# A planned linear-attention and Fourier-mixing kernel: new load lengths in its plan, and the stored order of work and choice of engines made anew

## The chip, the core and the metric

The kernel runs on one core of a Trainium2 chip. The metric is device time in microseconds (us) of one execution. The kernel before takes 182.72 us, the median of three runs (182.53 to 183.22). About 0.5% of that, 0.9 us, is what a measurement of this kernel can tell from no change.

## The reference

Two stages follow each other, on 4 batches of 768 positions and 8 heads of 48 columns (384 columns in all). The first is a linear attention with a decaying state, the second a Fourier mixing of the whole batch and a two-layer network.

```python
for t in range(S):                                   # S = 768
    cur = einsum('bhd,bhe->bhde', u[None] * kt, vt)
    y[:, :, t] = einsum('bhd,bhde->bhe', rt, state + cur)
    state = wt[:, :, :, None] * state + einsum('bhd,bhe->bhde', kt, vt)
x = y as (batch, position, 384)
mixed = real(fft(fft(x, axis=1), axis=2))
u = x + mixed
un = (u - mean(u)) / sqrt(var(u) + 1e-06)            # over the 384 columns
out = u + maximum(un @ w_ch1, 0.0) @ w_ch2           # 384 -> 1536 -> 384
```

Inputs and output are float32; the kernel multiplies in bfloat16.

## The kernel before

**Tiling.** A batch is cut into six chunks of 128 positions, so that a tile is 128 positions by 384 columns. Chunk c of batch b is written (b, c) here. For each chunk, SP loads four tiles: `w`, `k`, `r` and `v`, of 192 KB each (`load_one`, L606). Seven buffers of each kind are used in turn. That makes 96 loads. The bonus `u` is one small load, the two network weights come in three large transfers issued by POOL (`weights`, L742).

**Attention** (`attention(b, c)`, L757). ACT takes the logarithm of `w` (tile `lb`), PE sums it along the positions by two matmuls with triangular masks (L773, L777), ACT exponentiates both sums (L779, L792). DVE multiplies `r` by one (L811) and DVE or POOL multiply `k` by the other (`rkh`, recorded by the helper line L561). Both are transposed on PE (L827, L833) and copied out of the accumulators (`rkt`). In batch 3 a DMA transposes them. PE multiplies them (L843), DVE masks the product (`ah`, L848), PE multiplies it with `v` and adds the state's part (L896, L899). The diagonal term goes a side way: `rk` = r times k, times u, a row sum (`dc`, L800), times v (`vtd`). The result is a row block of `x`. PE, DVE and at times ACT move the state to the next chunk (L869, L877, tile `st`).

**Fold** (`fold`, L914). Sums and differences of `x` (tiles `sd`, `xf`), on DVE or POOL, put it into the even and odd parts that halve the transform.

**Mixing and network** (`mix(b)`, L944). PE multiplies the folded tiles with cosine and sine tables (L965 to L968), the results are copied (`hcs`) and mirrored (`hcr`), and multiplied with the second table (L992). DVE adds `x` and takes row sums (L997). ACT or DVE make the centred tile `un`, which is transposed (`unt`). Two halves of three row blocks then go through the network: 12 groups of three matmuls of 128x384 (L1056), each followed by the rectifier that writes `ht` either on ACT (L1064) or on DVE (L1062), and 12 matmuls for each row block (L1075), scaled and added by DVE (`osb`, L1081) and stored by SP (L1085).

**What sets the order.** The program is recorded as 1450 numbered steps. `ORDER` (L40) holds for each engine the numbers of its steps, in the order in which it runs them; the list in which a number stands is also the choice of engine, for steps that have a choice. Each engine runs its list strictly in order, and waits on semaphores where a step needs something from another engine. `schedule` (L205) walks through these lists with planned lengths of steps. It decides three things that reach the chip: which of the eight accumulator banks a tile gets, the waits which follow from a bank's reuse, and some waits of POOL on DVE. It does not change the lists. The planned length of a load is `xfer=960` ns (L611), and the same number marks the loads for the rule that no more than four are under way in the plan (L240 and L293).

```python
L240    if e == "sp" and o.sem is not None and len(lds) >= 4:
L241        s = max(s, lds[-4].end - 100)
L293    if o.xfer == 960:
L294        lds.append(o)
```

PE also runs 36 matmuls without use (`warm`, steps 1414 to 1449, L1130), placed by the list between useful ones. All stand ahead of the first network matmul. The kernel opens with 16 more on a memset tile (L1098).

**Overlap.** The lists weave the stages of neighbouring batches: while batch b is in attention, PE runs the mixing and network of batch b - 1 between its steps.

Of the kernel before, what the change touches and what calls it, by code (L numbers as in the profile page):

```python
# [66 lines left out]
    "act": (  # L67
# [14 lines left out]
    "dve": (  # L82
# [61 lines left out]
class _Prog:  # L144
# [60 lines left out]
    def schedule(self, order):  # L205
# [19 lines left out]
        for left in range(len(self.ops)):  # L225
            best = None
            for e in self.ENGS:
                if at[e] == len(self.order[e]):
                    continue
                o = self.order[e][at[e]]  # L230
# [9 lines left out]
                if e == "sp" and o.sem is not None and len(lds) >= 4:  # L240
                    s = max(s, lds[-4].end - 100)  # L241
# [48 lines left out]
            elif o.sem is not None:  # L290
                t = self._land(max(hw[-1][3] if hw else 0, s + o.set), o.xfer, sw)
                hw.append([s + o.set, o.xfer, o, t])
                if o.xfer == 960:  # L293
                    lds.append(o)  # L294
# [869 lines left out]
```

## Time and profile before

| | |
|---|---|
| median of three runs | 182.72 us (182.53 to 183.22) |
| profiled execution: own time | 184.21 us |
| its span, first to last instruction | 182.4 us |
| granted TensorE clock | 1.00 |
| bytes moved by DMA | 28.99 MB |

The profile comes from one execution. The span is what the profile's rows add up to; 1.8 us of that execution lie outside it. Times of rows count from the start of the span. A group of instructions stands in one row: source line, engine, operation, tiles and shapes, how often, then busy time and the mean duration of one instruction in ns, then the idle time of the engine ahead of them and what ended most of it. Instructions of DVE and ACT overlap a little at their ends, so that the mean duration is longer than the distance of two starts. "PE" rows show matmuls, whose ends are modelled. Where the trace shows a helper's line (L561 for a product or sum of two tensors, L575 for an activation, L586 and L587 for copies out of the accumulators), the tile's name tells which step it is.

### The profile page before, as it was taken

The numbers are of one execution on the slowest core, as the hardware profiler recorded it, in microseconds if no ns is written. First come the engines' busy times: TensorE is split into PE (matmuls) and PEld (weight loads), VectorE is DVE, ScalarE is ACT, GpSimd is POOL, SyncE is SP. The second block draws the span as 40 slices with busy tenths as digits, with TensorE's granted clock in tenths as the row PEclk, the third lists the DMA queues.
The fourth block names the chain that finished last, engine by engine and source line by source line (L and its number), as shares of the span: only waits on it lengthen the run. The fifth ranks groups of instructions, "written<-read, shape, count | busy, mean of one in ns | idle before, by whom it ended". The sixth has DMA issues, their size and how long they took to land.

```text
span 182.4 us, 4568 instructions
## 1 busy us (share of the span) xinstructions
PE 176.8 (97%) x1722; PEld 116.3 (64%) x1722; DVE 148.2 (81%) x341; ACT 130.2 (71%) x340; POOL 101.5 (56%) x120
## 2 busy tenths in 40 slices
PE   7999999999999999999999999999999999999994
PEld 3465676766566666776657666656666676666663
DVE  8779999899899999999888997899979927622343
ACT  2889859597898675799899978888882247478200
POOL 2448789767231498589998968769653440000000
DMA  4999998999999899999999999997550103331214
GB/s 97 203 216 196 208 191 172 185 202 208 152 196 190 162 210 230 226 204 182 202 222 218 219 177 207 220 212 179 103 114 0 47 2 65 73 125 43 86 71 145
DMA packets 116119, 28.99 MB, mean 159 GB/s; under 512 B 111361, under 2 KB 116098, under 8 KB 116098
## 3 DMA queue, kind: packets, MB, share of 16 engines
q1 hardware_dynamic: 114514, 26.36, 70.2%
q0 software_dynamic: 1584, 2.36, 8.0%
q8 instruction: 13, 0.21, 0.5%
q14 instruction: 8, 0.07, 0.1%
HBM read 23.59 MB, written 4.72 MB: 155 GB/s over the span
## 4 chain that ended last, share of the span: by engine, by line
PE 61%; DVE 17%; DMA 9%; SPq 4%; ACT 4%; issue 3%; DVEq 0%
PE bank L1075 18%; PE bank L1056 17%; DMA in_w<-in_w_dram 5%; DMA w<-in_moe_w_ch_dram 4%; DVE ah L848 4%; SPq L609 4%; PE bank L992 3%; PE bank L1130 3%; PE bank L1098 3%; PE bank L968 3%; DVE osb L1081 2%; PE bank L843 2%; DVE rkh L561 2%; PE bank L889 2%; PE bank L899 2%
## 5 line engine op out<-in xcount | busy, mean ns | idle before, releaser
L1075 PE MATMUL bank<-w,ht 128*128 128x384 bf16 (+2 forms) x300 | 53.7, 320 | 0.0
L1056 PE MATMUL bank<-unt,w 128*128 128x384 bf16 x288 | 51.9, 326 | 0.6 <-DMA w<-in_moe_w_ch_dram 0.6
L1064 ACT ACTIVATE ht<-bank 128x384 bf16<-128x384 f32 x72 | 32.6, 496 | 9.3 <-PE bank L1056 8.9
L1056 PEld LDWEIGHTS bank<-unt,w 128*128 128x128 bf16 x288 | 26.9, 98 | 17.5 <-DVE ht L1062 0.8
L1075 PEld LDWEIGHTS bank<-w,ht 128*128 128x128 bf16 x300 | 27.5, 98 | 15.2
L848 DVE TENSOR_TENSOR ah<-bank,msk 128x512 bf16<-128x512 f32 x48 | 31.2, 682 | 2.1 <-PE bank L843 2.0
L561 POOL TENSOR_TENSOR rk<-rk,ub 128x384 f32<-128x384 f32 x21 | 21.6, 1034 | 8.6 <-DVE rk L561 7.0
L561 POOL TENSOR_TENSOR vtd<-in_v,dc 128x384 f32<-128x384 f32 x20 | 16.7, 837 | 11.2 <-DVE dc L800 8.1
L1081 DVE SCALAR_TENSOR_TENSOR osb<-bank,rstd,uf 128x384 f32<-128x384 f32 (+2 forms) x25 | 14.8, 596 | 9.5 <-PE bank L1075 5.9
L1062 DVE TENSOR_SCALAR ht<-bank 128x384 bf16<-128x384 f32 x24 | 13.0, 549 | 6.9 <-PE bank L1056 6.8
L561 POOL TENSOR_TENSOR rk<-in_r,in_k 128x384 f32<-128x384 f32 x17 | 16.9, 999 | 2.9 <-DMA in_r<-in_r_dram 1.4
L997 DVE SCALAR_TENSOR_TENSOR uf<-bank,x 128x384 f32<-128x384 f32 x24 | 12.5, 553 | 4.7 <-PE bank L992 4.6
L561 POOL TENSOR_TENSOR rkh<-in_k,e 128x384 bf16<-128x384 f32 x14 | 14.1, 1009 | 3.6 <-ACT e L792 2.0
L779 ACT ACTIVATE bank<-bank 128x384 f32<-128x384 f32 x24 | 11.5, 484 | 5.8 <-PE bank L773 5.8
L811 DVE TENSOR_TENSOR rkh<-bank,in_r 128x384 bf16<-128x384 f32 x24 | 13.1, 549 | 2.1 <-ACT bank L779 2.0
L575 ACT ACTIVATE xf<-uf,agg 128x384 bf16<-128x384 f32 x24 | 14.7, 614 | 0.0
L561 POOL TENSOR_TENSOR xf<-sd 128x382 bf16<-128x382 f32 (+1 forms) x10 | 10.6, 1062 | 6.5 <-DVE sd L561 3.0
L575 ACT ACTIVATE lb<-in_w 128x384 bf16<-128x384 f32 x24 | 12.4, 519 | 2.1 <-DMA in_w<-in_w_dram 1.8
L575 ACT ACTIVATE un<-uf,agg 128x384 bf16<-128x384 f32 x18 | 10.6, 611 | 4.1 <-DVE uf L997 4.1
L586 ACT ACTIVATE rkt<-bank 128x256 f32<-128x256 f32 x29 | 10.8, 389 | 3.6 <-PE bank L833 2.4
L561 POOL TENSOR_TENSOR sd<-x 128x385 f32<-128x385 f32 x10 | 10.0, 1015 | 5.9 <-DVE x L908 5.4
L792 ACT ACTIVATE e<-bank 128x392 f32<-128x392 f32 (+1 forms) x24 | 11.7, 497 | 2.3 <-DVE bank L877 1.0
(138 smaller groups left out, 358.7 us busy)
## 6 DMA issues: line engine op xcount, KB each, us to landing
in_w<-in_w_dram SPq DMA_DIRECT2D x24, 192.0 KB, 3.8
in_k<-in_k_dram SPq DMA_DIRECT2D x24, 192.0 KB, 3.8
in_r<-in_r_dram SPq DMA_DIRECT2D x24, 192.0 KB, 4.1
in_v<-in_v_dram SPq DMA_DIRECT2D x24, 192.0 KB, 4.0
out_dram<-osb SPq DMA_DIRECT2D x23, 192.0 KB, 2.8
w<-in_moe_w_ch_dram POOLq DMA_DIRECT2D x2, 576.0 KB, 8.1
w<-in_moe_w_ch_dram POOLq DMA_DIRECT2D x1, 1152.0 KB, 10.7
out_dram<-osb SPq DMA_DIRECT2D x1, 128.0 KB, 1.7
```

The lines of the kernel that those rows point to most:

```text
L561: return lambda e: e.tensor_tensor(out=o, in0=a, in1=b, op=f)
L575: return lambda e: e.activation(o, a, f, **kw)
L779: op("act", a_ps(DM) + 20, lambda e: e.activation(ps(tce)[:, 0:DM], ps(tce)[:, 0:DM], ACTF.Exp), w=[tce])
L792: op("act", a_ps(ne), lambda e: e.activation(E2[i2][:, 0:ne], ps(tci)[:, 0:ne], ACTF.Exp), r=[tci], w=[("E2", i2)])
L811: op("dve", v_1(DM), lambda e: e.tensor_tensor(out=rh[:, :, 0:D], in0=ps(tce)[:, 0:DM].rearrange("t (h d) -> t h d", d=D), in1=rt[:, :, :] ...
L848: masked[n] = op("dve", v_1(512), lambda e, x=x: e.tensor_tensor(out=ah[:, x:H:2, :], in0=ps(ta[x])[:, :].rearrange("p (h t) -> p h t", t= ...
L997: op("dve", v_1(DM) + 60, lambda e, kb=kb, t=t: e.scalar_tensor_tensor(out=uf[:, kb, :], in0=ps(t)[:, 0:DM], scalar=1.0, in1=xb[:, kb, 0:D ...
L1056: ins = e.matmul(ps(t)[:, 0:384], W1[:, m, 256 * (j // 2) + j % 2:256 * (j // 2) + 256:2], unt[:, :, m, :], start=(m == 0), stop=(m == NM ...
L1062: {"dve": lambda e, j=j, t=t, ht=ht: e.tensor_scalar(out=ht[:, j, :], in0=ps(t)[:, 0:384], scalar1=su, scalar2=0.0, op0=ALU.mult, op1=ALU. ...
L1064: "act": lambda e, j=j, t=t, ht=ht: e.activation(ht[:, j, :], ps(t)[:, 0:384], ACTF.Relu, scale=su)},
L1075: ins = e.matmul(ps(t)[:, 0:hi - lo], ht[:, j, 128 * x:128 * x + 128], W2[:, j, lo:hi], start=(j == 0), stop=(j == NJ - 1))
L1081: op("dve", v_1(hi - lo) + 64, lambda e, kb=kb, t=t, o=o, lo=lo, hi=hi: e.scalar_tensor_tensor(out=o[:, lo:hi], in0=ps(t)[:, 0:hi - lo], s ...
```

## The change

Two lines of code change the planned length of a load: 920 ns in batch 0, 1030 ns in batches 1 to 3. And all five lists of `ORDER` are replaced by others. The set of steps is the same: 569 on PE, 132 on SP, 116 on POOL before and after. ACT has 300 instead of 316, DVE 333 instead of 317, since steps with a choice have moved: 44 from ACT to DVE and 31 from DVE to ACT, 23 from DVE to POOL and 26 from POOL to DVE, and three from ACT to POOL. The order of the loads differs too: SP's list begins with u, r(0,0), k(0,1), r(0,1), w(0,0), w(0,1), k(0,0), v(0,0) in place of w(0,1), u, w(0,0), k(0,0), r(0,0), k(0,1), v(0,0), r(0,1).

The diff, with the middle of each list cut:

```diff
 ORDER = {
     "pe": (
-        "7 1414 68 1415 1416 1417 1418 1419 1420 1421 1422 95 1423 94 121 122 97 124 62 64 1424 149 1425 151 "
...
+        "7 68 1414 1415 1416 1417 1418 1419 1420 95 94 1421 122 121 97 60 124 1422 1423 1424 64 62 176 1425 "
...
     "act": (
-        "0 17 18 19 93 120 96 123 98 125 147 103 63 174 152 109 55 65 135 56 136 61 130 150 201 179 163 117 "
...
+        "0 17 18 19 93 120 55 69 96 98 103 123 61 174 147 125 109 63 152 135 130 136 179 157 150 65 228 163 "
...
     "dve": (
-        "6 34 20 26 8 35 21 40 9 10 11 28 25 12 23 24 15 5 14 13 22 27 39 16 29 52 53 38 31 43 49 57 42 47 "
...
+        "25 23 6 26 45 43 8 20 32 10 11 9 37 58 12 38 5 13 22 15 14 41 28 24 16 31 27 59 30 29 21 49 39 50 "
...
     "pool": (
-        "145 199 226 252 227 262 460 253 454 46 483 484 455 425 254 457 513 486 547 515 584 549 579 532 531 "
...
+        "172 173 226 252 227 46 262 253 489 431 454 455 483 254 512 428 513 518 457 484 486 515 546 547 578 "
...
     "sp": (
-        "73 67 66 70 71 74 72 75 77 81 76 78 85 79 82 80 83 88 86 84 89 87 90 91 415 92 444 473 417 416 502 "
-        "445 446 474 475 504 536 418 447 503 476 538 569 537 505 571 570 539 846 759 572 788 762 761 370 760 "
...
+        "67 71 74 75 66 73 70 72 81 76 77 78 79 82 80 83 88 85 91 86 84 87 89 90 473 92 415 417 444 416 446 "
+        "445 502 474 447 536 475 418 503 476 504 537 505 569 538 571 570 759 788 539 761 846 572 790 370 365 "
...
@@ schedule
-                if o.xfer == 960:
+                if o.xfer in (920, 1030):
                     lds.append(o)
@@ load_one
-               w=[("in", n, i)], sem="in_%s%d" % (n, i), xfer=960)
+               w=[("in", n, i)], sem="in_%s%d" % (n, i), xfer=920 if b == 0 else 1030)
```

115 rows, old and new, of the table ORDER are left out of this document.

## The prediction

> **What bounds the kernel now.** I read the head of the profile's page first, for the span and the busy shares.
>
> ```profile
> span 182.4 us, 4568 instructions
> PE 176.8 (97%) x1722; PEld 116.3 (64%) x1722; DVE 148.2 (81%) x341; ACT 130.2 (71%) x340; POOL 101.5 (56%) x120
> ```
>
> PE looks full. Ends of matmuls are modelled, so I check this against distances of starts, in the chain that ended last.
>
> ```profile
> 37.82 8.02 DMA w<-in_moe_w_ch_dram
> 45.97 1.14 PE bank L1056 x6
> ...
> 91.41 0.52 ACT lb L575
> ...
> 92.90 0.34 PE bank L777
> ...
> 156.38 7.80 PE bank L1056 x48
> ...
> 179.92 0.35 DVE osb L1081
> ```
>
> 48 network matmuls of 384 columns take 7.80 us, 162.5 ns each. By that scale, columns over 384 times 162.5 ns, all of PE's instructions (those on float32 tiles taken four times, the smallest at 23 ns) come to 168.0 us. This is an estimate, and the same before and after, since the steps on PE are the same. 182.4 less 168.0 leaves 14.4 us in which PE does nothing it must: the head, the tail and small waits. PE is really near its bound, and a new order can win a few us of waits and no more.
>
> The Trainium skill says so as a rule ("Perfetto Trace Analysis", Identifying the Most-Contended Engine): PE's headroom isn't read from matmul busy time, since pipelined matmuls mislead. Here busy time says 5.6 us idle and the scale 14.4, so the trace agrees.
>
> Next the busy times of three stretches: attention of batch 0 and the start of the network, then the weave of batches 1 to 3, then the last batch's network.
>
> ```profile
> core 0: us, PE busy (x) PEld busy (x) DVE busy (x) ACT busy (x) POOL busy (x), PEclk, DMA share, GB/s
> 10.00:60.00 50.00, 49.04 (x556) 33.38 (x555) 46.46 (x100) 41.62 (x109) 30.48 (x37) 1.00 1.04 192
> 60.00:140.00 80.00, 79.30 (x861) 53.42 (x859) 74.26 (x157) 66.22 (x179) 62.59 (x66) 1.00 0.92 186
> 140.00:182.40 42.40, 39.81 (x278) 25.31 (x276) 20.28 (x45) 17.11 (x47) 4.41 (x4) 1.00 0.24 71
> ```
>
> The average of 81% for DVE hides two regimes. From 10 to 140 us DVE is busy for 120.72 of 130 us (93%); behind that for 20.28 of 42.40 (48%). In the weave PE and DVE are bound together: PE needs DVE's results just when they are ready. Two places in the timeline of DVE and PE near the end of the weave show it.
>
> ```profile
> 139.05 0.55 DVE L1062 TENSOR_SCALAR ht<-bank 128x384 bf16<-128x384 f32 x1
> 139.53 0.56 DVE L877 TENSOR_TENSOR st<-bank,e 128x384 bf16<-128x384 f32 x1
> ...
> 144.78 0.55 DVE L561 TENSOR_TENSOR sd<-x 128x385 f32<-128x385 f32 x1
> 145.44 0.56 DVE L561 TENSOR_TENSOR xf<-sd 128x384 bf16<-128x384 f32 x1
> 145.91 0.55 DVE L1062 TENSOR_SCALAR ht<-bank 128x384 bf16<-128x384 f32 x1
> 149.92 0.56 DVE L997 SCALAR_TENSOR_TENSOR uf<-bank,x 128x384 f32<-128x384 f32 x1 [3.46 <-PE bank L992]
> ...
> 146.19 0.25 PE L968 MATMUL bank<-ss,xf 128*128 128x193 bf16 x1
> ```
>
> DVE ends the last `sd` at 145.33, and the sine matmuls of batch 3, which need batch 3's fold, run from 146.19. Behind this DVE waits 3.46 us for PE. So up to about 146 us PE can't run ahead of DVE; from there to the end PE runs alone and densely.
>
> **The change part by part.** The new load lengths are no instructions. They reach the chip through banks and waits that the plan derives, and I give that no price of its own. What counts is the lists.
>
> *DVE gets more to do ahead of that place.* I take step 1269 as the mark, a sine matmul of batch 3 (the one at 146.19). In PE's new list 134.8 us of work by the scale above stand ahead of it, in the old 135.2: it has not moved. Following every wait back to DVE's list, the steps that DVE must have done by then are these, old against new: `sd` 8 and 12, `xf` of full width or its halves 11 and 16, `ht` 18 and 22, `hcs` 2 and 4, `rk` 10 and 6, `st` copied by itself 3 and 1. Their rows:
>
> ```profile
> L561 DVE TENSOR_TENSOR sd<-x 128x385 f32<-128x385 f32 x8 | 5.2, 665 | 0.1
> L561 DVE TENSOR_TENSOR xf<-sd 128x384 bf16<-128x384 f32 x6 | 3.5, 596 | 0.1
> L1062 DVE TENSOR_SCALAR ht<-bank 128x384 bf16<-128x384 f32 x24 | 13.0, 549 | 6.9 <-PE bank L1056 6.8
> L587 DVE CAST hcs<-bank 128x386 bf16<-128x386 f32 x2 | 1.2, 604 | 0.6 <-PE bank L966 0.6
> L561 DVE TENSOR_TENSOR rk<-in_r,in_k 128x384 f32<-128x384 f32 x7 | 4.3, 611 | 0.0
> L587 DVE CAST st<-bank 128x384 bf16<-128x384 f32 x3 | 1.7, 550 | 0.0
> L1064 ACT ACTIVATE ht<-bank 128x384 bf16<-128x384 f32 x72 | 32.6, 496 | 9.3 <-PE bank L1056 8.9
> ```
>
> The start after an `ht` at 139.05 is at 139.53: an instruction costs its mean less 0.07 us. So +4 `sd` at 0.60 is +2.4, +5 `xf` at 0.52 is +2.6, +4 `ht` at 0.48 is +1.9, +2 `hcs` at 0.54 is +1.1, -4 `rk` at 0.55 is -2.2, -2 `st` at 0.48 is -1.0. The small rest (`unt`, `hcr` and mirrored tables more; `osb`, `ub`, one `rkh` and fills fewer) is -0.7 by the same rule. Sum: **+4.1 us of DVE work ahead of the mark**. The work ACT is spared is off the path: its 66.22 of 80 us leave it room anyway.
>
> How much of this delays PE depends on DVE's idle time in the weave: 80 less 74.26 is 5.74 us. Its waits there:
>
> ```profile
> DVE ah L848 <- PE bank L843: 1.6, 3, 1.0
> DVE bank L877 <- PE bank L869: 0.9, 2, 0.5
> DVE x L908 <- PE bank L899: 0.7, 2, 0.4
> ```
>
> They are the round trips of the attention's chain, DVE to PE and back. Some go once DVE is the later one and its inputs lie ready; those where the next step needs the last one's result stay. No row tells the split. The bounds are 0 recovered (+4.1 on the path) and more than 4.1 recovered (0 on the path). I take half, 2.9 us: **+1.2 us**.
>
> *The first weight transfer's second half.* The chain's row at 37.82 begins with its issue, and PE goes on at 45.97, behind an idle of 0.6 us. In POOL's old list a `rkh` stands ahead of it:
>
> ```profile
> L1056 PE MATMUL bank<-unt,w 128*128 128x384 bf16 x288 | 51.9, 326 | 0.6 <-DMA w<-in_moe_w_ch_dram 0.6
> ...
> 36.10 1.00 POOL L561 TENSOR_TENSOR rkh<-in_k,e 128x384 bf16<-128x384 f32 x1
> 37.82 0.80 POOL L745 DMA_DIRECT2D w<-in_moe_w_ch_dram  x1 [0.73 <-DVE rkh L561]
> ```
>
> In the new list that `rkh` is gone from there and a memset of 0.41 us stands instead, so the issue comes up to 1.3 us earlier. The bounds are 0 and -0.6; I take -0.4, since the transfer queues behind the first half.
>
> *Loads.* In SP's list w(1,1) goes from the 27th to the 29th place, while PE's new list wants its sum (L777) about where PE stood at 31.2 us before. The 29th DMA before was this:
>
> ```profile
> 26.56 2.10 SPq L609 DMA_DIRECT2D in_r<-in_r_dram  x1
> in_r<-in_r_dram SPq DMA_DIRECT2D x24, 192.0 KB, 4.1
> L575 ACT ACTIVATE lb<-in_w 128x384 bf16<-128x384 f32 x24 | 12.4, 519 | 2.1 <-DMA in_w<-in_w_dram 1.8
> ```
>
> 26.56 plus 4.1 is 30.7, plus a logarithm of 0.52 and handing over: PE would wait until 31.5 or so. Bounds 0 (ACT and PE are both later by then) and +1; I take **+0.5**. On the other side w(2,5) moves forward by four places. Before, ACT waited for loads of `w` (1.8 us in all, the row above), the chain shows one such wait at 91.41, and PE's L777 starts only at 92.90. That is -0.5 to 0, but it lies in the weave, where DVE decides: 0.
>
> *The head.* w(0,0) goes from third to fifth place among the DMAs, but ACT only ends its table load at 7.40 us:
>
> ```profile
> 6.12 1.28 ACT L695 ACT_TABLE_LOAD   x1
> 7.50 0.52 ACT L575 ACTIVATE lb<-in_w 128x384 bf16<-128x384 f32 x1
> 2.82 1.47 SPq L609 DMA_DIRECT2D in_r<-in_r_dram  x1
> ```
>
> The fifth DMA was issued at 2.82; with the 4.1 us to landing above it is there at 6.9, ahead of 7.40. Price 0; the table load hides it. If that cover went, each load further back costs about 1 us. ACT then does a table copy and the bonus ahead of its exponentials, some 0.2 us later than before, while PE fills the place with its unused matmuls: 0, at most +0.5.
>
> *The tail.* ACT gives DVE more of batch 3's `ht` (549 ns for 496). DVE is busy there for 20.28 of 42.40 us. Its whole new list is 7.9 us longer, 3.8 of it behind the mark: it fits. The last matmuls and the last store are unchanged: 0. POOL has fewer `sd` and `xf` behind the weave and more products in its first half; with 62.59 of 80 us it isn't the bound: 0.
>
> **Sum**: +1.2 - 0.4 + 0.5 = +1.3 us. The span would go from 182.4 to 183.7. The profiled execution took 184.21 in all, 1.8 around its span; the median of the three runs is 182.72, and I add the difference to that: **184.0 us**.
>
> **The rivals.**
>
> *DVE is full, and takes nothing back.* Then all 4.1 us are late at the mark, and behind it PE has some 33 us of dense work, so they stay to the end: 182.72 + 4.1 = 186.8. For it: the weave's DVE has no long wait to give up; the longest is 1.0 us. Against: each wait in the list is for another engine. The Trainium skill ("Perfetto Trace Analysis", Optimizing Scalar/DVE Operations) advises, where DVE is saturated, to hand work that either can do to ScalarE; this change does the reverse, 44 steps to DVE against 31. By that rule 186.8 would be the time. The busy rows agree that DVE is the fuller one, 74.26 against 66.22 in the weave.
>
> *DVE closes its gaps, and the waits for DMA go.* This is the other side. If DVE's idle time between 60 us and the mark falls under about 1.6 us (5.74 less 4.1), PE is never late, and the weight wait (-0.6) and the wait at 91.41 to 92.90 (about -0.7) are won: 181.4. For it: from 100 to 110 us of the run DVE idles not at all, and the lists were made with load lengths nearer to what the trace shows. Against: 1.6 us in 86 is about a quarter of its idle rate now.
>
> ```profile
> 100.00:110.00 10.00, 10.00 (x108) 6.42 (x107) 10.00 (x21) 8.92 (x26) 7.61 (x9) 1.00 1.15 200
> ```
>
> *r(1,3) lands behind the last weight transfer.*
>
> ```profile
> w<-in_moe_w_ch_dram POOLq DMA_DIRECT2D x1, 1152.0 KB, 10.7
> ```
>
> In the new list r(1,3) stands as the 41st DMA, before as the 36th, and PE wants its product at about 57.8. The large transfer holds loads back for most of its 10.7 us. If it gets ahead of r(1,3), PE waits about 2 us near 58, on top of the forecast: about 186. It decides by whether POOL's issue of that transfer comes before r(1,3) is under way.
>
> *No difference.* The two lists balance: about 182.7, with DVE recovering 4.0 of 5.74. That would also hold if only labels moved; but lists do differ on every engine.
>
> **How the numbers follow.** Forecast 0.40; DVE full 0.14; r(1,3) late 0.08; these are slower by over 0.9 us (0.5%, what a measurement can tell): 0.62. No difference 0.16. Waits gone 0.22. The forecast's own range is 183.6 to 185.5, for a recovery of DVE's idle time from 58% down to 25%. The whole range reaches to 181.4 less 0.2 for the lower rival's unknowns, and to 186.8: 181.2 to 186.8.
>
> **What would show it.** Right: DVE busy from 60 to 140 us above 76 us, its idle there about halved, the last fold's product ending near 147 instead of 145.33, PE's own waits in the weave up by 1 to 2 us, and a dense PE behind. The wait at 45.97 gone or shorter. Wrong: DVE's busy time in the weave not up, or up with the mark still at 146; a new long wait of PE for a load or for POOL; or a tail where PE waits for `ht` on DVE.

## The result, and the profile after

The changed kernel takes 183.88 us (median of 20 runs, 182.65 to 184.58), the kernel before 182.69 us in the runs beside it (20 runs, 181.54 to 183.51). The ratio is 1.0063, with a 95% interval of 1.0043 to 1.0083: 0.8 to 1.5 us slower. The predicted 184.0 us was met, but by luck: the experiments below show that most of its reason was wrong. The time isn't lost to DVE in the weave. Most of it is lost ahead of the weave, and the new order of the loads is what costs it.

The profiled execution of the changed kernel took 183.35 us, with a span of 181.5. All lines of the code moved up by one: L574 is the old L575, L1055 the old L1056. First the head of the page, then the three stretches.

```profile
span 181.5 us, 4564 instructions
PE 175.9 (97%) x1722; PEld 115.2 (63%) x1722; DVE 153.1 (84%) x357; ACT 124.3 (68%) x324; POOL 101.3 (56%) x120
...
10.00:60.00 50.00, 49.09 (x553) 32.61 (x552) 45.96 (x100) 39.76 (x104) 33.95 (x41) 1.00 1.07 200
60.00:140.00 80.00, 79.61 (x864) 53.61 (x862) 76.18 (x164) 65.27 (x177) 62.01 (x65) 1.00 0.88 177
140.00:181.50 41.50, 38.96 (x263) 24.74 (x261) 23.35 (x54) 12.74 (x35) 1.65 (x2) 1.00 0.26 77
```

DVE is busy for 76.18 of the 80 us, as forecast (above 76, from 74.26); its idle time there fell by a third, from 5.74 to 3.82, not by half. But this row depends on the execution as much as on the lists: later profiles show 75.77 for the changed kernel (number 5) and 75.44 for the old lists (number 6).

The forecast counted DVE's extra work with the durations of the old kernel, and these did not stay. The first two lines below are of the changed kernel, the last two of the kernel before:

```profile
L560 DVE TENSOR_TENSOR sd<-x 128x385 f32<-128x385 f32 x12 | 6.4, 559 | 0.0
L560 POOL TENSOR_TENSOR sd<-x 128x385 f32<-128x385 f32 x6 | 6.3, 1051 | 1.0 <-DVE x L907 0.9
...
L561 POOL TENSOR_TENSOR sd<-x 128x385 f32<-128x385 f32 x10 | 10.0, 1015 | 5.9 <-DVE x L908 5.4 <-DVE sd L561 0.5
141.53 1.12 DVE L561 TENSOR_TENSOR sd<-x 128x385 f32<-128x385 f32 x1
```

DVE's `sd` takes 559 ns on average now and took 665 before. Of the eight before, five took 548 to 561 ns and three took 643, 795 and 1120 ns; while each of those three ran, POOL ran a sum or product too (from 141.23 to 142.23 us beside the one shown). One of the five ran beside POOL as well and took 549 ns, so what exactly makes them longer stays open. In the new lists POOL has six `sd` instead of ten, and all twelve of DVE's take 552 to 603 ns. DVE's `xf`, `rkh` (k's) and `vtd` got shorter on average too. Added up by the prediction's rule, but with each instruction's own duration, DVE's work ahead of the mark (step 1269) is 132.6 us before and 133.3 us after: +0.6 us where the forecast had +4.1. Numbers 6 and 5 below give 132.2 and 133.0, +0.8. Over all profiles it is 132.2 to 133.5 with the old lists and no added work, and 132.2 to 133.3 with the new lists on DVE, PE, ACT and POOL.

Now the place that was to be late, batch 3's fold, in the timeline of DVE and PE:

```profile
142.40 1.02 DVE L560 TENSOR_TENSOR xf<-sd 128x382 bf16<-128x382 f32 x2
143.33 0.55 DVE L1061 TENSOR_SCALAR ht<-bank 128x384 bf16<-128x384 f32 x1
143.80 0.55 DVE L560 TENSOR_TENSOR xf<-sd 128x382 bf16<-128x382 f32 x1
...
144.87 0.59 PE L967 MATMUL bank<-ss,xf 128*128 128x193 bf16 x5
```

The mark, step 1269, starts at 144.95, in the row of five sine matmuls. Before, it was 146.19. This is the wrong direction for a kernel that is 1.2 us slower, and a warning: the profiled execution of the kernel before took 184.21 us, longer than all 20 of its timed runs, while that of the changed one lies 0.5 us below its own median. These two traces can't carry a difference of 1 us. A better pair came later, from two profiles on one chip (numbers 5 and 6) whose times lie 0.1 and 0.6 us below the medians of their kernels.

What else the trace of the changed kernel says:

```profile
L1055 PE MATMUL bank<-unt,w 128*128 128x384 bf16 x288 | 54.2, 326 | 0.0
L1061 DVE TENSOR_SCALAR ht<-bank 128x384 bf16<-128x384 f32 x35 | 18.6, 551 | 6.9 <-PE bank L1055 6.8
L574 ACT ACTIVATE lb<-in_w 128x384 bf16<-128x384 f32 x24 | 12.1, 519 | 2.2 <-DMA in_w<-in_w_dram 2.1
```

PE no longer waits for the first weights (0.0 in the first row, 0.6 before). ACT's waits for `w` come to 2.1 us, little more than the 1.8 before, but they have another place:

```profile
12.66 0.52 ACT L574 ACTIVATE lb<-in_w 128x384 bf16<-128x384 f32 x1 [0.89 <-DMA in_w<-in_w_dram]
30.69 0.52 ACT L574 ACTIVATE lb<-in_w 128x384 bf16<-128x384 f32 x1 [1.23 <-DMA in_w<-in_w_dram]
```

These are w(0,2) and w(1,1), both in the first 31 us. I had looked at the second only.

### The profile page after: what moved, and what is told of

Its sections match the earlier page's. It is cut to its first block, busy times and chain, and to the rows that moved or that the text cites. A ratio compares the mean times of both kernels' runs of the same rounds, so it can differ in the third digit from the quotient of the medians.

```text
span 181.5 us, 4564 instructions
## 1 busy us (share of the span) xinstructions
PE 175.9 (97%) x1722; PEld 115.2 (63%) x1722; DVE 153.1 (84%) x357; ACT 124.3 (68%) x324; POOL 101.3 (56%) x120
## 4 chain that ended last, share of the span: by engine, by line
PE 86%; DVE 5%; SPq 4%; DMA 2%; ACT 1%; issue 1%; DVEq 0%
PE bank L1074 25%; PE bank L1055 24%; PE bank L991 6%; PE bank L967 5%; SPq L608 4%; PE bank L842 4%; PE bank L898 2%; DMA in_w<-in_w_dram 2%; PE bank L888 2%; PE bank L832 2%; PE bank L1129 2%; PE bank L826 2%; PE bank L868 2%; PE bank L895 2%; PE bank L772 2%; PE bank L776 2%
## 5 line engine op out<-in xcount | busy, mean ns | idle before, releaser
L1055 PE MATMUL bank<-unt,w 128*128 128x384 bf16 x288 | 54.2, 326 | 0.0
L1063 ACT ACTIVATE ht<-bank 128x384 bf16<-128x384 f32 x61 | 27.9, 489 | 15.9 <-PE bank L1055 15.6
L1055 PEld LDWEIGHTS bank<-unt,w 128*128 128x128 bf16 x288 | 26.5, 98 | 15.7 <-DVE unt L586 0.4
L1061 DVE TENSOR_SCALAR ht<-bank 128x384 bf16<-128x384 f32 x35 | 18.6, 551 | 6.9 <-PE bank L1055 6.8
L560 POOL TENSOR_TENSOR rk<-in_r,in_k 128x384 f32<-128x384 f32 x20 | 20.5, 1026 | 6.6 <-DMA in_r<-in_r_dram 4.4
L560 POOL TENSOR_TENSOR rk<-rk,ub 128x384 f32<-128x384 f32 x22 | 22.4, 1019 | 1.2 <-DVE rk L560 0.5
L560 POOL TENSOR_TENSOR rkh<-in_k,e 128x384 bf16<-128x384 f32 x15 | 15.1, 1009 | 7.4 <-ACT e L791 4.6
L574 ACT ACTIVATE xf<-uf,agg 128x384 bf16<-128x384 f32 x24 | 14.6, 611 | 0.8 <-DVE uf L996 0.8
L574 ACT ACTIVATE lb<-in_w 128x384 bf16<-128x384 f32 x24 | 12.1, 519 | 2.2 <-DMA in_w<-in_w_dram 2.1
L799 DVE TENSOR_REDUCE dc<-rk 128x8 f32<-128x384 f32 x24 | 12.7, 541 | 0.0
L574 ACT ACTIVATE vb<-in_v 128x384 bf16<-128x384 f32 x22 | 11.2, 519 | 0.8 <-DMA in_v<-in_v_dram 0.7
L574 ACT ACTIVATE un<-uf,agg 128x384 bf16<-128x384 f32 x18 | 10.2, 609 | 2.2 <-DVE uf L996 2.2
```

Of the source, the lines that this page charges most:

```text
L560: return lambda e: e.tensor_tensor(out=o, in0=a, in1=b, op=f)
L574: return lambda e: e.activation(o, a, f, **kw)
L799: op("dve", v_1(DM), lambda e: e.tensor_reduce(out=dc[:, :], in_=rku[:, :, :], axis=mybir.AxisListType.X, op=ALU.add), r=[("RK", i2)], w=[ ...
L1055: ins = e.matmul(ps(t)[:, 0:384], W1[:, m, 256 * (j // 2) + j % 2:256 * (j // 2) + 256:2], unt[:, :, m, :], start=(m == 0), stop=(m == NM ...
L1061: {"dve": lambda e, j=j, t=t, ht=ht: e.tensor_scalar(out=ht[:, j, :], in0=ps(t)[:, 0:384], scalar1=su, scalar2=0.0, op0=ALU.mult, op1=ALU. ...
L1063: "act": lambda e, j=j, t=t, ht=ht: e.activation(ht[:, j, :], ps(t)[:, 0:384], ACTF.Relu, scale=su)},
```

## The experiments

The first four ran on a chip on which everything took longer: the kernel before had a median of 185.31 us there, with runs from 183.61 to 191.31. The others ran on three chips on which it took 182.42, 182.14 and 182.23 us. Each ratio below is to the kernel before on the same chip. Verdicts that need less than 0.5% rest on the later runs.

**1. The kernel before, again** (no edit).

> The kernel before once more, for a second profile and the spread. All theories: 182.7 us, ratio 1.000 within 0.3%. The first profile of before took 184.21 us, longer than any of its 20 timed runs (181.54 to 183.51), so its span of 182.4 us is expected to be about 1.5 us above the one of this profile (near 180.9 us); the place where the two profiles of the same program part tells what varies.

Measured: 1.0013 (0.997 to 1.0056). The mark came at 147.66 in its profile, 1.5 us later than in the first profile of the same program. So much for what one execution says.

**2. New lengths, old lists.**

```diff
-                if o.xfer == 960:
+                if o.xfer in (920, 1030):
...
-               w=[("in", n, i)], sem="in_%s%d" % (n, i), xfer=960)
+               w=[("in", n, i)], sem="in_%s%d" % (n, i), xfer=920 if b == 0 else 1030)
```

> The lists of before with the new load lengths: every engine's steps stand in the old order, only banks and the waits that the plan derives change. Theory 1 (the lists give DVE more work ahead of batch 3's fold, and that is late): no change, 182.7 us, ratio 1.000. Theory 2 (the loss comes from the banks and waits that the plan derives): up to 183.9 us, ratio near 1.006.

Measured: 1.005 (1.0009 to 1.0091), which speaks for theory 2. But the profile puts the loss on a load. In DVE's and PE's timeline:

```profile
55.46 0.56 DVE L561 TENSOR_TENSOR rk<-in_r,in_k 128x384 f32<-128x384 f32 x1 [1.86 <-DMA in_k<-in_k_dram]
...
56.55 0.34 PE L869 MATMUL bank<-vb,rkh 128*128 128x96 bf16 x4 [1.00 <-DVE st L587]
```

A tile of `k` was issued at 45.74 here, at 44.93 in the copy of the old kernel and at 44.32 in its first profile, with the same list of loads. Whether the new numbers of banks lead to that or chance, one profile can't say; number 6 is the same program on another chip.

**3. New lists, old lengths** (the inverse edit on the changed kernel).

> The new lists with the old load length of 960 ns: the other half of the change alone. Theory 1: as the changed kernel, 183.9 us, ratio 1.006, with DVE busy above 76 us between 60 and 140 us. Theory 2: nearer to 182.7 us, ratio under 1.003.

Measured: 1.0037 (0.9995 to 1.008). It decides nothing by itself. Its profile shows ACT waiting five times for loads between 8 and 34 us, 3.93 us in all.

**4. Nine needless reductions on DVE, old lists.**

```diff
+    for i in range(9):
+        op("dve", 0, lambda e, i=i: e.tensor_reduce(out=DUM[:, i, :], in_=UB[:, :, :], axis=mybir.AxisListType.X, op=ALU.add),
+           r=["UB"], w=[("DUM", i)])
```

> The kernel before with nine row sums without use on DVE (tensor_reduce of the bonus tile, 0.47 us each from start to start, 4.2 us in all), spread from 64 to 128 us of its run; lists, banks and waits otherwise as before. Theory 1: part of the 4.2 us reaches the end, 0.25 to 0.75 of it, 183.8 to 185.9 us (ratio 1.006 to 1.017). Theory 1 in its strong form (DVE full): 186.9 us. Theory 2 (DVE has room in the weave): at most 183.2 us, ratio under 1.003.

Measured: 1.0052 (0.9996 to 1.0107), so between nothing and 2 us for 4.2 us of work. Too wide to tell the theories apart; number 11 doubles the dose on a quieter chip.

**5. The changed kernel, again** (no edit), to be compared with 6 to 8.

> The changed kernel unaltered, as the measure for the three others of this comparison. Both theories: 1.006 of the kernel before (1.004 to 1.008, as measured), some +1.2 us. Theory 1 (more DVE work ahead of batch 3's fold, +4.1 us): the sine matmul that serves as mark, at the same work of PE, starts 0.8 to 1.5 us later than in the fastest profile of the kernel before. Theory 2 (loads and the first 60 us decide): at 52 us of PE's own work the changed kernel is already 1 us later and no later behind that.

Measured: 183.76 us, 1.0085 (1.005 to 1.0121). Its profiled execution took 183.63 us.

**6. New lengths, old lists, again** (the program of number 2).

> The old lists with the new load lengths once more (only numbers of accumulator banks and a few places of waits differ; all steps stand on the same engines in the same order), on another chip, since the first comparison gave 1.005 but its profile showed a load of k that was issued 1.4 us later than in the copy of the old kernel, and DVE waiting 1.86 us for it. If the banks and waits cost (theory 2): 1.003 to 1.006 again, and a wait of PE near 55 us of 1 us again. If that was an accident of the loads (theory 1): 1.000, within 0.002, and the wait is not there or lies elsewhere.

Measured: 182.67 us, 1.0008 (0.9977 to 1.0039), and no wait near 55 us. Here the lengths alone, with the banks and waits that follow from them, have no price that shows. Number 2 had a load delayed in its profile; whether that explains its 1.005 isn't shown. Its profiled execution took 182.06 us, so it also serves as the profile of the old lists on this chip.

**7. New lists first, then old ones.** Each engine's list begins with the steps that the new plan starts in its first 57.5 us, in the new order and on the new engine; all others follow by the old lists.

```diff
-ORDER = (lists of before)
+ORDER = (lists of after, steps started before 57.5 us of its plan) + (lists of before, all other steps)
```

> The new lists for all steps that the plan starts in its first 57.5 us (the tables, attention of batch 0 and the first part of batch 0's network, and the loads in that time), then the old order and the old choice of engine for all the others; the old lengths. DVE has 0.3 us more than before to do ahead of the mark instead of 4.1. Theory 1 (DVE work ahead of the mark): 0.999 to 1.002, since the excess is gone; DVE busy from 60 to 140 us 73 to 75. Theory 2 (the new first part with its loads is what costs): 1.004 to 1.007, as the changed kernel. A price of the seam of up to 0.5 us can lie on top in both.

**8. Old lists first, then new ones**, with the cut at 80 us.

```diff
-ORDER = (lists of after)
+ORDER = (lists of before, steps started before 80 us of its plan) + (lists of after, all other steps)
```

> The old lists for all steps that the plan starts in its first 80 us, then the new order and the new choice of engine for the others; the new lengths. DVE has 3.4 us more than before to do ahead of the mark. Theory 1: 1.003 to 1.007 (half or more of the excess late at the mark, +0.6 to +1.3 us); DVE busy from 60 to 140 us 75 to 77. Theory 2 (the new first part costs): 0.999 to 1.002. A price of the seam of up to 1 us can lie on top in both, to be seen as a wait of PE near 80 us.

Measured: number 7 takes 184.81 us, 1.0133 (1.0083 to 1.0183); number 8 takes 182.65 us, 1.0004 (0.9976 to 1.0031). That turns theory 1 over. Seven has no more DVE work ahead of the mark than the kernel before (+0.3 us) and takes the longest. Eight has +3.4 us of it by the prediction's count, and by its own durations 133.4 us (132.2 in number 6, 133.0 in number 5), and takes no longer than before that shows; the lower end of theory 1, 1.003, just touches its interval. What costs is the first 57 us. (That seven comes out even above the changed kernel may be its seam or chance: the intervals overlap.) The weave, 60 to 140 us, of seven and then of eight:

```profile
60.00:140.00 80.00, 79.69 (x855) 53.69 (x854) 74.25 (x160) 66.26 (x181) 62.56 (x66) 1.00 0.88 182
...
60.00:140.00 80.00, 79.52 (x867) 53.14 (x866) 75.67 (x162) 65.19 (x177) 60.28 (x64) 1.00 0.89 177
```

Seven has the emptier DVE there (74.25), eight the fuller one (75.67), and the times go the other way.

Where the time is lost shows when PE reaches the same amount of its own work (columns over 384 times 160 ns, the figure with which the prediction's sums come out), in us. The first three rows are from one chip; number 9, told below, ran on another:

| PE's own work done | 20 | 36 | 52 | 60 | 100 | 132 |
|---|---|---|---|---|---|---|
| old lists (6) | 26.39 | 42.64 | 59.03 | 67.54 | 108.26 | 140.92 |
| old then new (8) | 26.03 | 42.34 | 58.66 | 67.17 | 108.78 | 141.66 |
| changed (5) | 26.51 | 42.99 | 59.97 | 68.77 | 109.72 | 142.44 |
| 5 less 6 | 0.12 | 0.35 | 0.94 | 1.23 | 1.46 | 1.52 |
| changed, loads sorted (9) | 25.98 | 42.47 | 58.86 | 67.65 | 108.59 | 140.86 |

Of the 1.5 us between 5 and 6, 1.2 are lost by 69 us; the whole rest of the weave adds 0.3. The two executions differ by 1.57 us, their kernels' medians by 1.09, so some of this is chance. Theory 2 of number 5 had 1 us by 52 us of PE's work (0.94 is there) and nothing behind it (0.6 is). Between 60 and 132 us of its work eight loses 1.1 us against six, 0.6 of it by 80, where its seam lies. The changed lists in 5 and 9 lose at most 0.3 there, so this isn't put down to them.

A cause lies between 8 and 34 us. ACT's waits for DMA there, in the profile of 5; the profile of 6 has none:

```profile
ACT lb L574 <- DMA in_w<-in_w_dram: 2.0, 3, 0.9
ACT vb L574 <- DMA in_v<-in_v_dram: 0.4, 1, 0.4
```

The chain that ended last, between 8 and 34 us, by line, for 5 and then for 6:

```profile
by line: SPq L608 24.0%; DMA in_w<-in_w_dram 17.8%; PE bank L1129 9.3%; PE bank L888 9.0%; PE bank L967 6.1%; PE bank L842 5.1%; ACT lb L574 3.7%; PE bank L826 3.2%; PE bank L898 2.9%; PE bank L772 2.9%; PE bank L895 2.7%; ACT rkt L585 2.1%
...
by line: PE bank L1130 17.8%; PE bank L889 13.2%; PE bank L843 6.2%; PE bank L968 5.8%; PE bank L773 4.9%; ACT e L792 4.5%; PE bank L899 4.4%; ACT dtm L740 4.4%; PE bank L827 4.4%; PE bank L777 3.8%; PE bank L896 3.4%; ACT bank L779 3.3%; A
```

In the changed kernel 42% of the chain in this stretch is the queue of loads and the landing of `w`; in the old order no load lies on it. Most profiles say the same: loads and their queue hold 18, 77, 42 and 56% of it in the four that begin with the changed kernel's lists, and nothing in five of the seven that begin with the old ones. The other two, 46% in number 1 and 48% in number 2, are from the chip of the first four runs.

In 5 the last of these loads on the chain lands at 18.72, and by 43 us only 0.35 us are lost. The next 0.9 us come between 43 and 69 us, where no load is on the chain of either. That the late loads set off this part too is argued, not shown. What they may have left to DVE, busy from 18 to 34 us, 5 and then 6:

```profile
18.00:34.00 16.00, 15.70 (x212) 10.89 (x210) 13.88 (x29) 12.43 (x32) 13.52 (x17) 1.00 1.03 202
18.00:34.00 16.00, 16.00 (x216) 11.46 (x215) 15.37 (x32) 11.77 (x31) 14.55 (x18) 1.00 1.05 208
```

DVE is busy for 1.5 us less there (13.88 against 15.37), with the DMA equally full in both (1.03 and 1.05). At 45.9 and 47.5 us PE then waits, 0.5 us in all, for the network's first `un` and `unt`, which DVE makes; the profile of 9 doesn't have this wait. Loads land at the same pace, one about every 0.95 us; it is the order that differs. In the trace of 5, nine of the first 29 loads land within 0.15 us of the start of their first user; in that of 6, none. These two are the ends of a spread: such loads number 0 to 5 in the seven profiles that begin with the old lists, 6 to 9 in the four that begin with the changed kernel's. ACT's waits for loads between 8 and 34 us come to 0 to 0.45 us in the seven, and to 2.12, 2.39, 2.87 and 3.93 us in the four.

The plan shows why these loads have no slack. For four loads of 5, its times and the chip's, in us:

| load | place | lands: plan | lands: trace | first use: plan | first use: trace |
|---|---|---|---|---|---|
| w(0,2) | 11 | 12.24 | 12.12 | 12.29 | 12.14 |
| w(0,5) | 17 | 17.76 | 18.72 | 18.09 | 18.74 |
| w(1,0) | 27 | 27.18 | 28.00 | 27.23 | 28.03 |
| w(1,1) | 29 | 29.24 | 30.25 | 29.29 | 30.27 |

With 920 ns for each load of batch 0 the plan has them land too early, by 0.4 to 1.3 us for all from the 16th to the 29th, and the new order uses three of these four within 0.05 us of the planned landing. On the chip a single load is late by about 1 us somewhere (in 5 it is the 16th, which lands 2.0 us after the 15th), and all behind it up to the 29th stay late by 0.4 us or more.

**9. Loads sorted.** The changed kernel with its 9th to 34th load (SP's list) in the order in which their first users started in the profile of 5.

```diff
-67 71 74 75 66 73 70 72 81 76 77 78 79 82 80 83 88 85 91 86 84 87 89 90 473 92 415 417 444 416 446 445 502 474 ...
+67 71 74 75 66 73 70 72 81 77 76 78 79 80 82 83 88 85 84 91 86 87 89 90 415 473 92 444 417 445 446 502 474 416 ...
```

> The changed kernel with its 9th to 34th load put in the order in which their first users started in its second profile; nothing else is altered but a few numbers of banks. There, nine of the first 29 loads landed within 0.15 us of their first use, and ACT waited 2.0 us for loads of w between 8 and 34 us, where the old lists had no such wait. By the landing times of the same places, w(0,2), v(0,3), w(1,0) and w(1,1) would now be there 0.9 to 2.5 us ahead of their use; w(0,5), r(0,3) and k(0,0) stay as late as they were. Theory 3 (the new order of loads leaves no slack, and PE pays for it in the first 45 us): 1.000 to 1.005 of the kernel before, 0.4 to 1.2 us less than the changed kernel (1.0063 and 1.0085 so far); ACT's wait for w between 8 and 34 us below 1.1 us. Theory 2 (what costs in the first part is the order of the steps on the engines, not the loads): as the changed kernel, 1.006 to 1.009.

Measured: 182.37 us, 1.0022 (0.9995 to 1.0048). Both signs of theory 3 are there: the time, and ACT's wait for `w` of 0.8 us, under 1.1. With nothing but the loads in another order (and a few banks that follow from it) the loss is gone down to what can't be told from none, and the new choice of engines stays. It is one run of 12 executions, and its interval still overlaps a little with the changed kernel's first one (from 1.0043) and with that of number 10 on the same chip (from 1.0041). Six of its first 29 loads still land within 0.15 us of their first use, so that count alone doesn't say what a kernel takes. Its chain between 8 and 34 us has no load on it, and its DVE is as full in the weave as the changed kernel's:

```profile
by line: PE bank L1129 15.7%; PE bank L888 14.7%; PE bank L842 7.6%; PE bank L832 6.3%; PE bank L967 6.1%; PE bank L826 5.3%; ACT lb L574 5.2%; PE bank L776 5.0%; PE bank L772 4.6%; PE bank L898 4.4%; PE bank L895 3.4%; PE bank L868 3.3%; A
...
ACT lb L574 <- DMA in_w<-in_w_dram: 0.8, 1, 0.8
...
60.00:140.00 80.00, 79.61 (x865) 53.70 (x863) 76.17 (x165) 64.30 (x173) 60.71 (x64) 1.00 0.86 177
```

**10. Two loads forward.**

```diff
-... 87 89 90 473 92 415 417 444 416 ...
+... 87 89 90 415 444 473 92 417 416 ...
```

> The changed kernel with only w(1,0) and w(1,1) moved forward, from the 27th and 29th place of the loads to the 25th and 26th (w(1,2) and v(0,5) and r(1,0) go back for them). Theory 3 with the price that the prediction put on w(1,1): 0.3 to 0.6 us less than the changed kernel, 1.004 to 1.006 of the kernel before, and no wait of ACT for w near 30 us (0.90 to 2.18 us in the profiles of the new lists so far). Theory 2: as the changed kernel, 1.006 to 1.009, though the wait is gone.

Measured: 183.52 us, 1.0064 (1.0041 to 1.0088). ACT's wait near 30 us is gone, and the time is as in the changed kernel: the price I had put on w(1,1) alone doesn't show, though up to 0.4 us of it would fit the interval. ACT's waits for loads between 8 and 34 us come to 0.9 us in all, little more than the 0.8 of number 9, so it isn't their sum that sets the time. Loads hold 18% of the chain there, as in the first profile of the changed kernel.

**11. Eighteen needless reductions on DVE, old lists** (as number 4, `range(18)`, a slot of `DUM` for each two).

> The kernel before with 18 needless reductions on DVE between 62 and 131 us, some 0.47 us each, 8.5 us in all, twice as many as in the earlier run with nine; lists, banks and waits of all else as before. DVE had 5.74 us idle in its profiled 80 us of the weave. Theory 1 (DVE and PE are bound together, half of the idle time can be recovered): 8.5 less 2.9 is +5.6 us, 1.03; at the very least 8.5 less 5.7, +2.8 us, 1.015. Theory 3 (PE alone decides in the weave; DVE's work has room of some us and only then hurts): 1.005 to 1.015, DVE idle in the weave below 2 us.

Measured: 185.93 us, 1.02 (1.0174 to 1.0225): +3.6 us for 18 reductions, which by the rule of the prediction (mean less 0.07 us) are 18 x 0.475 = 8.5 us. So 4.9 us of it were taken back. The row of the reductions, the weave, and the chain of the whole execution:

```profile
L1135 DVE TENSOR_REDUCE dum<-ub 128x8 f32<-128x384 f32 x18 | 9.8, 545 | 0.0
...
60.00:140.00 80.00, 78.27 (x828) 51.21 (x827) 78.76 (x172) 65.67 (x176) 61.74 (x65) 1.00 0.89 180
...
PE 51%; DVE 37%; ACT 3%; issue 3%; DMA 2%; POOL 2%; DVEq 0%; POOLq 0%; ACTq 0%
```

DVE's idle time fell to 1.24 us of 80, and DVE holds 37% of the chain, where it had 17% in the first profile of the old kernel and 7% in number 6. It was neither theory's case exactly: above the 0.5 to 1.5% of theory 3, within what theory 1 allowed (at least 1.5%), but far from its +5.6 us. DVE's room was some 5 us. The 4.1 us of the forecast would have fitted into it; what DVE in fact got more to do, at most 0.8 us, fits all the more.

**12. Early loads only.** Of number 9, only the edits up to the 24th place.

```diff
-... 72 81 76 77 78 79 82 80 83 88 85 91 86 84 87 89 90 473 ...
+... 72 81 77 76 78 79 80 82 83 88 85 84 91 86 87 89 90 473 ...
```

> The changed kernel with only the first of the two groups of edits that gave back 1.1 us together: w(0,2) one place forward (v(0,1) back), v(0,2) one place forward (k(0,3) back), v(0,3) from the 21st to the 19th place (v(0,4) and k(0,4) back). The 25th to 34th load stay as in the changed kernel. Moving w(1,0) and w(1,1) alone gave nothing (1.0064). Theory 3a (the price lies in the loads of batch 0, which land just at their use in the first 23 us): 1.001 to 1.004, all or most of the 1.1 us back. Theory 3b (no single place: what is won on an early load is lost again at the next late one, w(1,0) and w(1,1), so that both groups are needed): 1.005 to 1.008, and ACT's wait for w near 30 us longer than the 0.90 us of the changed kernel's second profile.

Measured: 183.24 us, 1.0062 (1.0028 to 1.0096), as the changed kernel, though the upper end of theory 3a (1.004) is inside the interval. The wait near 30 us is 0.35 us in its profile, not longer than 0.90, so theory 3b has the time right and not the place. Its profile still has late loads on ACT, and loads hold 34% of its chain between 8 and 34 us:

```profile
18.79 0.52 ACT L574 ACTIVATE lb<-in_w 128x384 bf16<-128x384 f32 x1 [0.83 <-DMA in_w<-in_w_dram]
28.61 0.94 ACT L574 ACTIVATE lb<-in_w 128x384 bf16<-128x384 f32 x2 [0.35 <-DMA in_w<-in_w_dram]
```

Neither group of edits shows a gain by itself; all of number 9 together does. Which of its moves from the 25th place on is needed beside the early ones (k(1,1) and k(1,0) change places there too) stays open.

No version beat the kernel before: numbers 8 and 9 come level with it.

## Why the prediction was right, and where it was not

**DVE and PE bound together in the weave, +1.2 us: wrong.** Two steps of it failed. The first is the size of DVE's extra work: the count of instructions was right, and with the old kernel's mean durations it comes to about 4 us, but on the chip DVE's work ahead of the mark grew by 0.6 to 0.8 us, as its `sd` went from 665 to 559 ns. DVE's busy time over the whole run grew by 4.9 us (148.2 to 153.1), where I had its list 7.9 us longer. The second is the share of DVE's idle time that it can take back: I took half, 2.9 of 5.74 us. Number 11 shows 4.9 us taken back, down to 1.24 us of idle time in 80, and number 8, with 1.2 us more of DVE's work ahead of the mark than number 6 by its own durations, changes the time by -0.4 to +0.6 us. PE's busy time in the weave didn't fall (79.61 us for 79.30). At the fold, `sd` ends even earlier than in the old order, at 142.76 in the profile of 5 and at 143.22 in that of 6. The last `xf` ends at 144.62, 0.6 us ahead of the mark, in 5, and at 143.89, 0.2 us ahead of it, in 6; nothing like the forecast 147. PE reaches the mark 1.15 us later, 145.23 for 144.08. My size for the lateness at the mark was right by luck; DVE wasn't its cause, PE had lost most of the time before the weave. The rule of the Trainium skill ("Perfetto Trace Analysis", Optimizing Scalar/DVE Operations) to relieve a saturated DVE, which would have given 186.8, isn't put to the test by the changed lists, whose DVE got hardly more to do. Where DVE really got more (number 11, busy for 78.76 of 80 us), 3.6 of 8.5 us reached the end.

**Loads: the right place, the wrong size.** I priced one load, w(1,1), at +0.5 us, and the head at 0 because the table load covered w(0,0). That cover was there: ACT's first logarithm starts at 7.48 in the profile of 5, at 7.50 in the trace of before. But I asked of only two loads when they land and when they are wanted. In the profile of 5 nine had no slack. Number 9 shows what their order costs: 1.0022 for 1.0063 and 1.0085, so 0.7 to 1.1 us, most of the loss, where I had +0.5 for one of them. How the late loads turn into PE's lost time, most of it behind 43 us, is argued. Moving w(1,0) and w(1,1) alone gives nothing back that shows (number 10).

**The first weights, -0.4 us: not a gain.** The wait at 45.97 went, but it was a feature of the execution that I read. PE's idle time around it (36 to 44 us of its own work) is 0.50 to 1.25 us in five profiles that begin with the old lists and 0.24 and 0.17 us in two more (6 and 8); with the new lists it is 0.1 to 0.9 us in four.

**Lengths without a price of their own: right on the chip** (number 6), but they did reach the time in another way, through the order of loads that was made with them. I had named that as a point for the opposite rival, "lengths nearer to what the trace shows". This is argued from the table of planned and real landings; no run made the lists anew with other lengths.

**PE near its bound, the tail and r(1,3)**: right. The scale of PE's work was off in a detail: the prediction names 162.5 ns for 384 columns, and the starts of such matmuls in the trace of before do lie 162 to 163 ns apart, but its sums (168.0, 134.8 and 135.2 us) come out with 160 ns. With 162.5 they are 170.4, 136.6 and 137.0, and 12.0 us are left over instead of 14.4. Nothing that follows hangs on that. From 140 us of PE's work to the end of the span it takes 31.2 us in every profile, with old lists and new. r(1,3) landed at 47.87 in the profile of 5, and PE has no wait for its product near 57 us.

**The sum**: +1.3 us forecast, +1.2 measured. The two agree by luck: +1.2 came from a term that is about nothing, and the loads, which cost most of it, stood in the sum with +0.5.

## What to carry to other kernels

For a static order, list for each load the landing time and the start of its first user, before and after: an order of loads without slack can cost a time that no other part of the change explains (0.7 to 1.1 us here), and no single load need show it. Idle time of an engine that is scattered in small waits for another one can be taken back for the most part (4.9 of 5.74 us here, where I had said half), so added work well below that sum shouldn't be priced at half of it; what 4.2 us of it cost, number 4 leaves open between 0 and 2 us. Work that moves between engines may not keep its duration: check the row of the same step after the change. And before reading a difference of 1 us from two traces, compare each profiled execution with the median of its kernel.

## What was not expected of the hardware

Loads of 192 KB land about every 0.95 us in the first 26 us, and yet single ones come 1 us late, at a place that changes from execution to execution (the 16th load in the profile of 5, the 26th in the first profile of the kernel before, which landed at 28.86 where the 25th had landed at 26.31). The same sum on DVE takes 548 ns or up to 1120 ns in one execution, the long ones while POOL runs such a step too. Two profiles of the same program (the kernel before and number 1) differ by 1.5 us at the mark. At 60 us of PE's work they are still within 0.2 us of each other, so the late loads of the first 26 us aren't what sets them apart; what does stays open.
